# Moving the sums of the weights to earlier places in a fused attention and mixer kernel on one Trainium2 core

## The chip, the cores and the metric

The kernel runs on one core of one Trainium2 chip. The metric is the device time of one execution in microseconds (us). Five engines run side by side, each with its own in-order queue: PE (TensorE: matmuls, with weight loads shown as PEld), DVE (VectorE), ACT (ScalarE), POOL (GpSimd) and SP (SyncE), which here only issues DMAs.

## The reference, cut to what matters

```python
def _attn_ref(q, k, v, mem_k, mem_v):             # q, k, v: 4 x 8 x 768 x 64
    for c in range(24):                           # chunks of 32 queries
        k_full = concat(mem_k, k[c_start - 16 : c_end + 8])   # 8 memory keys first
        a = softmax(q_c @ k_full.T / 8)           # denominator + 1e-9
        out[:, :, c_start:c_end] = a @ v_full

def _moe_ref(x, U, V, w_ch1, w_ch2):              # x: 4 x 768 x 512
    h = x.transpose(0, 2, 1) @ U @ V              # rank 32 over the sequence
    u = x + h.transpose(0, 2, 1)
    ch = np.maximum(u @ w_ch1, 0.0) @ w_ch2       # 512 -> 2048 -> 512
    return u + ch
```

The output of the attention, with its heads laid side by side, is the input x of the mixer. U, V, w_ch1 and w_ch2 arrive as 64-bit floats.

## The kernel before, in words

The four batches run one after another. A batch's mixer has two blocks of 384 tokens. The 2048 hidden columns are cut in 16 units of 128 (f = 0 to 15), two of which make a pair p. Each product is done in three passes over high and low parts of its operands (names ending in h and l), so a unit costs twelve matmuls into a hidden bank (`ps_h`), then a split of the ReLU of the bank into `hh` (ACT, L1254 or L1414) and `hl` (DVE, L1255 or L1415), then `w2_step`: six matmuls with hh and three with hl into the accumulators `acc`. There are two hidden banks and two buffers each of hh and hl.

**Batch 0** is plain: 32 units in `both_blocks`. The weights are decoded during it, each unit's w1 to a high part `w1h` that stays in SBUF and a low part `w1l` that is written to DRAM (`w1s`, `w1x`) and fetched again by SP when wanted, into a ring of five tiles. The last six units (n = 26 to 31) are f = 15, 14, 10, 11, 12, 13 of block 1.

**Batches 1 to 3** use a seven-product scheme in the manner of Strassen (`sevens`): for a pair, seven products of half size serve both blocks. It needs sums and differences of quarters of w1, the weights' sums, four for each pair, made once and kept in DRAM. `keep_sums` makes them from two whole w1 tiles: `whole` (POOL, L453) adds w1h and w1l of each, POOL does four additions (L463), ACT casts each of the four results to a high part (L466) and DVE subtracts to get the low part (L467); `save_sums` then lets SP write the four tiles to DRAM (L472). The tiles `homes` of a pair are the same as those of the pair ahead, so a cast can only write when the DMA that saved the pair ahead has landed.

**Where the sums are made before.** In batch 1, pairs 0 to 4 (`NPL = 5`) run their first block's product plain (the loop over `few = 10` units: `half_of`, the second half, the split, the `w2_step` of the unit ahead), since their sums do not exist yet. Beside it `late_sums` makes the sums of pairs 5, 6 and 7: it fetches their w1l again from DRAM into `vbs[1]` and works there. Pairs 5 to 7 then run as seven products. In the second half of batch 1, `other_half` adds two products to what was kept for each of the ten plain units, and makes the sums of pairs 0 to 4 from the very tiles that it multiplies with (`both`, L453 on `w1l`). The second half ends with w2 units alone.

**What else runs beside.** `attention(b + 1)` is a generator whose pieces (transposes of kn and qn, scores `kall,qt`, exponentials `pt`, transposes `ident,pt`, products `vb,pT`, the rank-32 chain) are put between the mixer's steps by calls of `give`. When they are used up, `give` takes pieces of `seven_u(b + 1)`, which turns the next batch's x (`ident,x`) into `uc` and makes the operands bh, bl, t12, t34 and b22 from it. For batch 1 these pieces are taken by hand near the end of the plain loop.

**What sets the order.** PE and SP run in the order in which the program is written. ACT, DVE and POOL are put in order by the framework's scheduler, except in marked stretches.

The lines that matter most below:

```python
if few:
    half_of(0)
    for _ in gen[0]: pass          # the last pieces of batch 1's attention
    ...
    for f in range(few):           # second half, split, half_of(f + 1), w2_step of the unit ahead
        ...
        if f == 0: last_step()     # w2_step of batch 0's last unit
        else: w2_step(b, 0, *prev, go)
```

Of the kernel before, what the change touches and what calls it, by code (L numbers as in the profile page):

```python
# [45 lines left out]
LASTW = 13  # L46
RING = 4
# [10 lines left out]
def chunk_attn_then_mixer_kernel(  # L58
# [418 lines left out]
    def late_sums():  # L477

        work = vbs[1].rearrange("c i d -> c (i d)")
        lows = [work[:, 512 * n:512 * n + 512] for n in range(2)]  # L480

        def fetch(p):
            for n in range(2):
                load_w1l(2 * p + n, lows[n].rearrange("p (c n) -> p c n", c=NCK))

        def make(p):
            for n in range(2):
                whole(lows[n], w1h[2 * p + n].rearrange("p c n -> p (c n)"), lows[n])
            keep_sums(p, *lows, [work[:, 1024:1536], work[:, 1536:2048]] + [slot([P, 512], F32, "sums") for _ in range(2)])

        for p in range(NPL, NF // 2):
            for step in (fetch, None, make, None, None, None):
                if step is not None:
                    step(p)
                yield
            save_sums()
# [697 lines left out]

    def list_items(b):
# [33 lines left out]
    def sevens(b, give, following, last_step=None):  # L1229
# [44 lines left out]
        prev, more = None, late_sums() if few else iter(())  # L1274

        def go():
            give()
            next(more, None)

        if few:  # L1280
# [11 lines left out]
            for f in range(few):  # L1292
                if f == 1:
                    send()
                six(banks[f], w1h[f][:, 2:4], lows.pop(f)[:, 1], 1, False)
                h = split(banks.pop(f)[:, :TOK])
# [5 lines left out]
                if f + 2 == few:  # L1302
                    closing.enter_context(tc.manual_schedule(engines=CLOSING))
                for _ in range(max(0, min(2, f + 4 - few))):
                    next(coming[0])
                go()
                if f + 1 < few:
                    half_of(f + 1)
                if f == 0:
                    last_step()  # L1310
                else:
                    w2_step(b, 0, *prev, go)
                if f + 3 >= few:
                    next(coming[0])
                prev = (f, 0, f == 0, None) + h
            for _ in more:
                pass
            held_w.close()
            seven["pools"][1].append(ctx.enter_context(tc.tile_pool(name="su2", bufs=1, side="right", reuse_waits="tile")))
        for p in range(few // 2, NF // 2):  # L1320
# [5 lines left out]
            last = p + 1 == NF // 2  # L1326
            xb, yb = hidden_bank(), hidden_bank()
# [291 lines left out]
```

## Time and profile before

| | us |
|---|---|
| median of 3 runs | 664.64 (664.52 to 665.15) |
| the profiled execution | 663.14 |
| its span, first to last instruction | 661.4 |
| PE busy | 635.6 (96%) |
| DVE, ACT, POOL busy | 362.3, 249.5, 84.6 |

PE is busy in all but a few stretches, so the time is the sum of PE's work and of the moments when PE has to wait. A wait on another engine matters only where PE is late because of it. In batch 0's last units, batch 1's plain part and its second half (170 to 380 us) the waits of PE can be read one by one; from 380 us to the last units PE does not wait.

### The profile page before, as it was taken

The numbers are of one execution on the slowest core, as the hardware profiler recorded it, in microseconds if no ns is written. First come the engines' busy times: TensorE is split into PE (matmuls) and PEld (weight loads), VectorE is DVE, ScalarE is ACT, GpSimd is POOL, SyncE is SP. The second block draws the span as 40 slices with busy tenths as digits, with TensorE's granted clock in tenths as the row PEclk, the third lists the DMA queues.
The fourth block names the chain that finished last, engine by engine and source line by source line (L and its number), as shares of the span: only waits on it lengthen the run. The fifth ranks groups of instructions, "written<-read, shape, count | busy, mean of one in ns | idle before, by whom it ended". The sixth has DMA issues, their size and how long they took to land.

```text
span 661.4 us, 15256 instructions
## 1 busy us (share of the span) xinstructions
PE 635.6 (96%) x6171; PEld 552.7 (84%) x6174; DVE 362.3 (55%) x703; ACT 249.5 (38%) x605; POOL 84.6 (13%) x114
## 2 busy tenths in 40 slices
PE   7698999999899999999999999999999999999997
PEld 5557999988787897898788699999978899999886
DVE  5948788898654536644577733443536732222322
ACT  5526344457323365533233516342224512122221
POOL 5100000042000335101666000000000000000000
PEclk9899999999999999999999999999999999999999
DMA  8994577765572696846565369675523046555301
GB/s 242 171 365 153 170 248 246 222 188 142 98 176 55 190 264 193 212 135 167 178 221 185 134 206 279 202 183 150 150 60 128 1 145 185 156 159 160 105 0 49
DMA packets 127150, 110.32 MB, mean 167 GB/s; under 512 B 51720, under 2 KB 97928, under 8 KB 127080
## 3 DMA queue, kind: packets, MB, share of 16 engines
q1 hardware_dynamic: 126456, 109.20, 57.1%
q8 instruction: 49, 0.80, 0.5%
q10 hardware_dynamic: 624, 0.15, 0.1%
q14 instruction: 21, 0.17, 0.1%
HBM read 86.11 MB, written 22.68 MB: 164 GB/s over the span
## 4 chain that ended last, share of the span: by engine, by line
PE 63%; DMA 4%; DVE 4%; ACT 2%; issue 1%; POOL 1%; SPq 0%; ACTq 0%; DVEq 0%; POOLq 0%
PE ps_h L1240 25%; PE acc L1457 18%; PE acc L1467 9%; PE ps_a L715 2%; DMA w1s<-both 2%; PE ps_h L1406 2%; PE acc L1451 2%; PE ps_a L583 1%; PE ps_a L696 1%; PE ps_a L642 1%; PE ps_a L1139 1%; DMA vb<-w1s 1%; DMA vb<-in_v_dram 1%; PE ps_a L1044 1%; PE ps_a L744 1%
## 5 line engine op out<-in xcount | busy, mean ns | idle before, releaser
L1457 PE MATMUL acc<-w,hh 128*128 128x512 f32 x612 | 158.5, 394 | 2.2 <-ACT hh L1254 2.2
L1457 PEld LDWEIGHTS acc<-w,hh 128*128 128x128 f32 x612 | 112.9, 188 | 23.0 <-ACT hh L1254 3.3
L1467 PE MATMUL acc<-w,hl 128*128 128x512 f32 x306 | 88.0, 396 | 0.0
L1467 PEld LDWEIGHTS acc<-w,hl 128*128 128x128 f32 x306 | 56.3, 188 | 11.9 <-DVE hl L1255 0.4
L1240 PE MATMUL ps_h<-t12h,w1l 128*128 128x384 f32 x192 | 57.1, 348 | 1.0 <-DMA w1l<-w1s 1.0
L1240 PE MATMUL ps_h<-bh,w1l 128*128 128x384 f32 x192 | 52.6, 339 | 0.0
L1240 PE MATMUL ps_h<-t34h,w1l 128*128 128x384 f32 x152 | 46.6, 348 | 0.0
L1406 PE MATMUL ps_h<-uh,w1h 128*128 128x384 f32 x124 | 42.5, 347 | 2.2 <-ACT w1h L365 1.2
L1255 DVE SCALAR_TENSOR_TENSOR hl<-ps_h,hh 128x384 fp32r<-128x384 f32 x29 | 16.1, 555 | 46.7 <-ACT hh L1254 46.7
L1406 PE MATMUL ps_h<-ul,w1h 128*128 128x384 f32 x124 | 41.3, 337 | 0.4 <-DVE ul L1121 0.4
L1262 DVE TENSOR_TENSOR c<-ps_h,c 128x384 f32<-128x384 f32 x19 | 10.6, 557 | 56.8 <-PE ps_h L1240 56.8
L1240 PEld LDWEIGHTS ps_h<-t12h,w1l 128*128 128x128 f32 x192 | 35.3, 188 | 3.3 <-DVE hst L1262 1.9
L1240 PEld LDWEIGHTS ps_h<-bh,w1l 128*128 128x128 f32 x192 | 35.1, 188 | 0.8
L1240 PE MATMUL ps_h<-b,w1l 128*128 128x384 f32 x174 | 35.3, 338 | 0.0
L1254 ACT ACTIVATE hh<-ps_h 128x384 fp32r<-128x384 f32 x29 | 14.3, 494 | 53.3 <-PE ps_h L1240 51.9
L1262 DVE TENSOR_TENSOR hst<-ps_h,hst 128x384 f32<-128x384 f32 x36 | 19.9, 553 | 24.5 <-ACT hst L1266 19.4
L1255 DVE SCALAR_TENSOR_TENSOR hl<-hst,hh 128x384 fp32r<-128x384 f32 x36 | 21.1, 585 | 22.2 <-PE acc L1467 21.4
L1254 ACT ACTIVATE hh<-hst 128x384 fp32r<-128x384 f32 x36 | 18.9, 525 | 36.0 <-PE acc L1457 30.1
L1240 PE MATMUL ps_h<-t12l,w1l 128*128 128x384 f32 x96 | 32.4, 337 | 0.0
L1266 ACT COPY c<-ps_h 128x384 f32<-128x384 f32 x19 | 9.1, 480 | 61.1 <-PE ps_h L1240 61.1
L1240 PEld LDWEIGHTS ps_h<-b,w1l 128*128 128x128 f32 x174 | 30.8, 188 | 0.3 <-DMA w1l<-w1s 0.3
L1414 ACT ACTIVATE hh<-ps_h 128x384 fp32r<-128x384 f32 x31 | 15.2, 490 | 40.5 <-PE ps_h L1406 40.5
(240 smaller groups left out, 1258.9 us busy)
## 6 DMA issues: line engine op xcount, KB each, us to landing
w1l<-w1s SPq DMA_DIRECT2D x155, 256.0 KB
rw<-in_moe_w_ch_dram SPq DMA_DIRECT2D x14, 512.0 KB
qraw<-in_q_dram SPq DMA_DIRECT2D x24, 256.0 KB
out_dram<-x SPq DMA_DIRECT2D x24, 256.0 KB
vb<-in_v_dram SPq DMA_DIRECT2D x56, 98.0 KB
raw<-in_moe_w_ch_dram SPq DMA_DIRECT2D x20, 256.0 KB
w1s<-both SPq DMA_DIRECT2D x20, 256.0 KB
kraw<-in_k_dram SPq DMA_DIRECT2D x16, 256.0 KB
```

What stands on the lines that cost most here:

```text
L583: nc.tensor.transpose(out=psv[:, p, r, :], in_=half[:, r, 2 * p:2 * p + 2, :].rearrange("n h d -> n (h d)"), identity=ident,)
L715: nc.tensor.matmul(out=psv[g][CK * i:CK * i + CK, t, j], lhsT=pt[j % 2][rows, 2 * t + j // 2, CK * i:CK * i + CK], rhs=vt[rows, NI * t + i ...
L1240: nc.tensor.matmul(out=ps[:, :TOK], lhsT=w_, rhs=u, start=(start and m == 0), stop=(m == 5), skip_group_check=True,)
L1254: nc.scalar.activation(out=hh, in_=c, func=AF.Relu)
L1255: nc.vector.scalar_tensor_tensor(out=hl, in0=c, scalar=0.0, in1=hh.bitcast(F32), op0=ALU.max, op1=ALU.subtract,)
L1262: nc.vector.tensor_tensor(out=out, in0=ps[:, :TOK], in1=in1, op=ALU.add)
L1266: nc.scalar.copy(out=out, in_=ps[:, :TOK])
L1406: nc.tensor.matmul(out=ph[:, :TOK], lhsT=w[:, c, :], rhs=u[c], start=(m == 0), stop=(m + 1 == len(parts)),)
L1414: nc.scalar.activation(out=hh, in_=ph[:, :TOK], func=AF.Relu)
L1451: nc.tensor.matmul(out=acc[tt], lhsT=h[:, sl], rhs=w, start=False, stop=(m == 2))
L1457: nc.tensor.matmul(out=acc[tt], lhsT=h[:, sl], rhs=w, start=(begins and m == 0), stop=False,)
L1467: nc.tensor.matmul(out=acc[tt], lhsT=hl[:, sl], rhs=w2h[f], start=False, stop=ends is not None)
```

## The change

The table below says how the sums are spread. In the last six units of batch 0 and in the plain loop, `take_value` makes the whole tile right behind the unit's products, from the w1l that the unit has used, and calls `keep_sums` when both units of a pair are there. Nothing is fetched again for it. A ring tile of w1l is now also read by POOL before it can be filled again.

| pairs | sums made before | sums made now |
|---|---|---|
| 7, 5, 6 | plain part of batch 1 (`late_sums`) | last six units of batch 0 |
| 0, 1, 2, 3 | second half of batch 1 (`other_half`) | plain part of batch 1 |
| 4 | second half of batch 1 | second half of batch 1, first |

The saves of a pair's sums are issued when the next pair is complete. Batch 1's second half takes its units in another order (15, 8, 9, 0 to 7, 10 to 14). At batch 1's head `last_step` comes first, then two halves instead of one. There is one call of `give` fewer ahead of the plain loop's end and the calls in pairs 5 to 7 stand at other places, so pieces of the attention move by one place. The pieces of `seven_u(1)` are taken in other units (`NEXTS`). Batch 1's first three output tiles are sent at n == 2 of the second half instead of when they are ready.

```diff
+NEXTS = {3: (1, 1), 2: (2, 3), 1: (1, 1)}
...
-    def late_sums():
...
+    def take_value(f, w1l, homes):
+        p, odd = divmod(f, 2)
+        values[f] = homes(f % 2)
+        whole(values[f], *(w.rearrange("p c n -> p (c n)") for w in (w1h[f], w1l)))
+        if 2 * p in values and 2 * p + 1 in values:
             save_sums()
+            keep_sums(p, values.pop(2 * p), values.pop(2 * p + 1), [homes(2 + n) for n in range(4)])
+    def slot_home(n):
+        return slot([P, 512], F32, "sums")
+    def work_home(n):
+        return vbs[1].rearrange("c i d -> c (i d)")[:, 512 * n:512 * n + 512] if n < 4 else slot_home(n)
...
+    def others(few):
+        return list(range(few - 2, few)) + list(range(few - 2)) if few else []
...
+            def other(f):
+                low = lows.pop(f)
+                six(banks[f], w1h[f][:, 2:4], low[:, 1], 1, False)
+                if f < few - 2:
+                    take_value(f, low.rearrange("p i c n -> p (i c) n"), work_home)
+                return split(banks.pop(f)[:, :TOK])
+            last_step()
             half_of(0)
+            half_of(1)
             for _ in gen[0]:
                 pass
             gen[0] = attention(b + 1, xs)
-            for f in range(few):
+            prev = (0, 0, True, None) + other(0)
+            for f in range(1, few):
+                h = other(f)
...
-                if f + 2 == few:
+                if f + 1 == few:
                     closing.enter_context(tc.manual_schedule(engines=CLOSING))
-                for _ in range(max(0, min(2, f + 4 - few))):
+                early, late = NEXTS.get(few - f, (0, 0))
+                for _ in range(early):
                     next(coming[0])
-                go()
+                give()
                 if f + 1 < few:
                     half_of(f + 1)
-                if f == 0:
-                    last_step()
-                else:
-                    w2_step(b, 0, *prev, go)
-                if f + 3 >= few:
+                w2_step(b, 0, *prev, give)
+                for _ in range(late):
                     next(coming[0])
+                if f + 2 == few:
+                    save_sums()
...
             for z in range(2):
                 w = product(ps, 6 if z else 3, z == 0)
-                at = slice(2 * P * z, 2 * P * z + 2 * P)
-                whole(both[f % 2][:, at], *(w[:, n].rearrange("p c n -> p (c n)") for n in range(2)))
+                if f + 2 >= few:
+                    ...
...
-        for n, f in enumerate([NF - 1] + list(range(NF - 1))):
+        for n, f in enumerate(order):
             hid_ = split(kept(f))
...
+            if n == 2:
+                save_sums()
+                send()
...
-            if not (SEVEN <= b + 1 < B and t + TB >= NT):
+            if b != SEVEN and not (b + 1 < B and t + TB >= NT):
                 send()
...
             hid_ = w1_step(0, blk, f, w1l, between if n else joins)
+            if blk and f >= 2 * NPL:
+                take_value(f, w1l, slot_home if f >= NF - 2 else work_home)
```

On PE, at the place where batch 0 ends and batch 1 begins. Before (hl: last pass of unit 30's w2; w1h_877: unit 0's weights; g,v: the rank-32 chain of batch 1's attention):

```order
L1467 MATMUL acc_2683<-w_1869,hl 128x512
L1240 MATMUL ps_h<-bh,w1h_877 128x384
L1240 MATMUL ps_h<-bl,w1h_877 128x384
L1240 MATMUL ps_h<-bh,w1h_877 128x384
L1240 MATMUL ps_h<-bl,w1h_877 128x384
L1240 MATMUL ps_h<-bh,w1l 128x384 x2
L1044 MATMUL ps_a<-g_2920,v_111 128x512 x3
L1240 MATMUL ps_h<-bh,w1h_877 128x384
```

On PE at the same place now (w_1961: the w2 of batch 0's last unit):

```order
L1474 MATMUL acc_2703<-w_1869,hl 128x512
L1464 MATMUL acc_2701<-w_1961,hh 128x512 x2
L1464 MATMUL acc_2702<-w_1961,hh 128x512 x2
L1464 MATMUL acc_2703<-w_1961,hh 128x512 x2
L1474 MATMUL acc_2701<-w_1961,hl 128x512
L1474 MATMUL acc_2702<-w_1961,hl 128x512
L1474 MATMUL acc_2703<-w_1961,hl 128x512
L1240 MATMUL ps_h<-bh,w1h_877 128x384
```

The nine matmuls of batch 0's last w2 step now stand between unit 30's w2 and batch 1's first half, the first reader of bh and bl.

On ACT at that place. Before (g: the rank-32 chain; uc, bh: operands of batch 1; hst: the kept half):

```order
L1026 CAST g_2920<-ps_a 96x512
L1141 COPY uc<-ps_a 128x512
L1145 CAST bh<-uc 128x4x128
L1414 ACTIVATE hh<-ps_h 128x384
L1141 COPY uc<-ps_a 128x512
L1145 CAST bh<-uc 128x4x128
L1141 COPY uc<-ps_a 128x512
L1145 CAST bh<-uc 128x4x128
L1266 COPY hst_3022<-ps_h 128x384
```

On ACT now (vb_115 and sums: the homes of a pair's sums, here pair 6, then pair 0):

```order
L1023 CAST g_2960<-ps_a 96x512
L467 CAST vb_115<-vb_115 128x256 x2
L1138 COPY uc<-ps_a 128x512
L467 CAST sums<-vb_115 128x256 x2
L1142 CAST bh<-uc 128x4x128
L1421 ACTIVATE hh<-ps_h 128x384
L1138 COPY uc<-ps_a 128x512
L1142 CAST bh<-uc 128x4x128
L1138 COPY uc<-ps_a 128x512
L1142 CAST bh<-uc 128x4x128
L467 CAST sums<-vb_115 128x256 x2
L1266 COPY hst_3082<-ps_h 128x384 x2
```

Six casts of sums now stand among the operands of batch 1, two of them ahead of the first uc.

On SP, in the second half of batch 1. Before (out_dram: batch 1's first three output tiles; w1l: ring tiles to come):

```order
L1199 DMA w1l<-w1s_126 128x512
L1432 DMA out_dram<-x 128x512 x3
L1199 DMA w1l<-w1s_127 128x512 x2
L1199 DMA w1l<-w1x_135 128x512
L1199 DMA w1l<-w1s_127 128x512
```

On SP now:

```order
L1199 DMA w1l<-w1s_127 128x512 x2
L1199 DMA w1l<-w1x_135 128x512
L1199 DMA w1l<-w1s_127 128x512
L473 DMA w1s_130<-both 128x512 x4
L1439 DMA out_dram<-x 128x512 x3
L1199 DMA w1l<-w1s_128 128x512 x2
```

The output tiles are sent eight ring tiles later (four of pair 4 stand ahead of those of pair 0), behind the saves of pair 4's sums.

## Rows read from the trace of the kernel before

**Rows 1.** Windows: us, busy PE PEld DVE ACT POOL (x count), PE clock, DMA, GB/s

```profile
170.00:205.00 35.00, 33.87 (x659) 27.63 (x658) 16.84 (x38) 8.85 (x19) 1.62 (x5) 1.00 0.63 135
220.00:250.00 30.00, 30.00 (x166) 27.20 (x165) 12.71 (x26) 15.12 (x47) 8.79 (x11) 1.00 0.84 244
358.00:374.00 16.00, 13.78 (x61) 10.16 (x60) 15.63 (x32) 8.97 (x21) 4.88 (x6) 1.00 0.58 197
490.00:532.00 42.00, 42.00 (x200) 34.75 (x199) 26.64 (x53) 18.30 (x35) 0.00 (x0) 1.00 0.15 51
```

**Rows 2.** Waits of PE: us in total, times, longest

```profile
PE ps_a L696 <- ACT pt L668: 2.5, 2, 1.6
PE acc L1457 <- ACT hh L1254: 2.2, 3, 1.1
...
PE ps_h L1240 <- DMA w1l<-w1s: 1.0, 1, 1.0
...
PE ps_h L1240 <- ACT bh L1145: 0.6, 1, 0.6
...
PE ps_h L1240 <- DVE bl L1129: 0.3, 1, 0.3
```

**Rows 3.** Timeline of ACT and DVE at batch 1's head: start, us, what

```profile
214.93 0.62 ACT L1145 CAST bh<-uc 128x512 fp32r<-128x512 f32 x1
215.57 0.69 DVE L1129 TENSOR_TENSOR bl<-uc,bh 128x512 fp32r<-128x512 f32 x1 [1.08 <-ACT bh L1145]
```

**Rows 4.** The chain that ended last, two pieces of batch 2: start, us

```profile
388.24 1.36 PE acc L1457 x6
390.28 2.10 PE ps_h L1240 x12
```

**Rows 5.** Timeline round the first exponentials of batch 2's attention

```profile
252.49 1.48 PE L642 MATMUL ps_a<-kall,qt 64*32 64x64 f32 x128
...
259.36 0.41 ACT L466 CAST vb<-vb 128x256 fp32r<-128x256 f32 x1 [3.62 <-POOL vb L463]
...
260.35 0.66 PE L696 MATMUL ps_a<-ident,pt 128*128 128x128 f32 x4 [1.60 <-ACT pt L668]
```

**Rows 6.** Timeline of PE round the third exponentials of batch 2's attention

```profile
302.79 1.49 PE L642 MATMUL ps_a<-kall,qt 64*32 64x64 f32 x128
...
307.47 0.66 PE L696 MATMUL ps_a<-ident,pt 128*128 128x128 f32 x4 [0.93 <-ACT pt L668]
```

**Rows 7.** Timeline of SP in the second half of batch 1

```profile
319.42 1.86 SPq L1432 DMA_DIRECT2D out_dram<-x  x3
```

**Rows 8.** Timeline of DVE and POOL near the end of batch 1

```profile
360.36 2.67 POOL L463 TENSOR_TENSOR both<-both 128x256 f32<-128x256 f32 x3
...
360.61 0.95 DVE L1167 TENSOR_TENSOR tb<-uc 128x256 f32<-128x256 f32 x1
...
369.54 0.41 DVE L1167 TENSOR_TENSOR tb<-uc 128x256 f32<-128x256 f32 x1
```

**Rows 9.** Groups by line and form: busy us, mean ns, idle before

```profile
...
L467 DVE TENSOR_TENSOR both<-both 128x256 fp32r<-128x256 f32 x20 | 10.3, 527 | 7.3 <-ACT both L466 7.2
...
L463 POOL TENSOR_TENSOR vb<-vb 128x256 f32<-128x256 f32 x12 | 9.2, 766 | 0.9
...
L466 ACT CAST both<-both 128x256 fp32r<-128x256 f32 x20 | 8.1, 405 | 17.6 <-DMA w1s<-both 12.2 <-POOL both L463 5.4
...
L453 POOL TENSOR_TENSOR vb<-w1h,vb 128x512 f32<-128x512 f32 x6 | 8.0, 1341 | 44.3 <-DMA vb<-w1s 44.3
```

**Rows 10.** Timeline of SP and POOL at batch 1's head: fetches and their reader

```profile
205.98 0.42 SPq L444 DMA_DIRECT2D w1l<-w1s  x1
...
214.96 0.42 SPq L444 DMA_DIRECT2D vb<-w1s  x1
...
217.59 2.56 POOL L453 TENSOR_TENSOR vb<-w1h,vb 128x512 f32<-128x512 f32 x2 [19.68 <-DMA vb<-w1s]
```

**Rows 11.** The chain, a piece of batch 1's second half

```profile
350.18 4.82 DMA w1s<-both
```

More of the change, by code (lines that the diff above doesn't have):

```diff
@@ L475, in save_sums @@
         unkept.clear()
-    def late_sums():
[L479 to L495, printed above, removed]
-            save_sums()
+    values = {}
+    def take_value(f, w1l, homes):
[3 more added lines that the diff above has]
+        if 2 * p in values and 2 * p + 1 in values:
+            save_sums()
+            keep_sums(p, values.pop(2 * p), values.pop(2 * p + 1), [homes(2 + n) for n in range(4)])
[3 more added lines that the diff above has]
+        return vbs[1].rearrange("c i d -> c (i d)")[:, 512 * n:512 * n + 512] if n < 4 else slot_home(n)
     def attention(b, xs):
@@ L1211, in list_items @@
         items.extend(whole_item(w1s_d[p][:, n]) for p in range(few // 2, NF // 2) for n in range(7))
-        for f in range(few):
+        for f in others(few):
             p, odd = divmod(f, 2)
@@ L1272, in hidden_bank @@
             return ps_h.tile([P, 512], F32, name="ps_h")
[L1274 to L1278, printed above, removed]
+        prev = None
         if few:
@@ L1291, in sevens @@
             gen[0] = attention(b + 1, xs)
-            for f in range(few):
+            prev = (0, 0, True, None) + other(0)
+            for f in range(1, few):
+                h = other(f)
                 if f == 1:
                     send()
-                six(banks[f], w1h[f][:, 2:4], lows.pop(f)[:, 1], 1, False)
-                h = split(banks.pop(f)[:, :TOK])
                 if f + 3 == few:
@@ L1326, in sevens @@
             last = p + 1 == NF // 2
+            even, other_places = (give, lambda: None) if few else (lambda: None, give)
             xb, yb = hidden_bank(), hidden_bank()
@@ L1330, in sevens @@
             keep(c11, xb)
+            even()
             product(yb, 1, True)
@@ L1334, in sevens @@
             if prev is not None:
-                next(coming[0])
+                for _ in coming[0]:
+                    pass
                 w2_step(b, 0, *prev)
                 prev = None
-                for _ in coming[0]:
-                    pass
                 coming[0] = seven_u(b + 1)
                 closing.close()
-            go()
+            other_places()
             product(xb, 2, False)
             keep(c12, xb)
-            go()
+            give()
             product(yb, 3, True)
-            go()
+            other_places()
             product(xb, 4, False)
@@ L1350, in sevens @@
             add(c22, yb, c22)
-            w2_step(b, 0, 2 * p, 0, 2 * p == 0, None, *h1, go)
-            go()
+            even()
+            w2_step(b, 0, 2 * p, 0, 2 * p == 0, None, *h1, other_places)
+            give()
             product(xb, 5, False)
@@ L1357, in sevens @@
             add(c12, yb, c12)
-            go()
-            w2_step(b, 0, 2 * p + 1, 0, False, True if last else None, *h2)
+            give()
+            w2_step(b, 0, 2 * p + 1, 0, False, True if last else None, *h2, even)
         if few:
@@ L1368, in other_half @@
                 w = product(ps, 6 if z else 3, z == 0)
-                at = slice(2 * P * z, 2 * P * z + 2 * P)
-                whole(both[f % 2][:, at], *(w[:, n].rearrange("p c n -> p (c n)") for n in range(2)))
+                if f + 2 >= few:
+                    at = slice(2 * P * z, 2 * P * z + 2 * P)
+                    whole(both[f % 2][:, at], *(w[:, n].rearrange("p c n -> p (c n)") for n in range(2)))
             add(kept(f), ps, kept(f))
-            if f % 2:
-                save_sums()
+            if f + 1 == few:
                 keep_sums(f // 2, both[0], both[1], both[2:])
-        for f in range(min(2, few)):
+        left = others(few)
+        order = [NF - 1] + left + list(range(few, NF - 1))
+        for f in left[:2]:
             other_half(f)
             give()
-        for n, f in enumerate([NF - 1] + list(range(NF - 1))):
+        for n, f in enumerate(order):
             hid_ = split(kept(f))
@@ L1386, in sevens @@
             if n + 2 < few:
-                other_half(n + 2)
+                other_half(left[n + 2])
                 if n < LATER:
@@ L1391, in sevens @@
                 w2_step(b, 1, *prev)
-            if n == 2 * LATER:
-                save_sums()
             prev = (f, 0, n == 0, True if n == NF - 1 else None) + hid_
```

4 lines of the change are left out of this document (1 added, 3 removed).

## The prediction

> **What bounds the kernel now.** I began with the page's busy shares: PE is busy 96% of the span, so the time is PE's work plus the moments in which PE stands. Then I read the granted clock in the windows, which is 1.00 in every stretch quoted [rows 1], the level of 2.4 GHz, so that no part of the time is a matter of the clock. Then came PE's waits from batch 1's head (205 us) to its end (374 us): the reader is to see that there are only a handful, 6.6 us together, each with its releaser [rows 2]: 2.5 for exponentials, 2.2 for splits, 1.0 for a fetch, 0.9 for the operands bh and bl. Last came the timelines round each of them. In batch 0's last units PE is busy 33.87 of 35 us, so another 1.1 us of waits stands there; what ends them (decodes of weights) is not touched, and I leave them in. From batch 2 on nothing is changed: PE's work is the same, and its waits start after the stretch.
>
> The profiled execution took 663.14 us (span 661.4, 1.74 around it); the median of the runs is 664.64, 1.50 above it. I make the sum against 663.14 and carry the 1.50 over.
>
> **What it removes and adds.** No matmul is added or removed; moved ones keep their length. So the time moves by PE's waits alone, and the gain can't be over the 6.6 us. Of other engines' work, six fetches for pairs 5 to 7 go (vb<-w1s, SP issue 0.42 us each [rows 10]). The sums themselves are only moved: for a pair four ACT casts of 0.405 us (1.6), four DVE subtractions of 0.527 (2.1), on POOL two wholes of 1.34 and four additions of 0.77 (5.8) [rows 9]. Three pairs come into batch 0's last units: 4.9 us of ACT, 6.3 of DVE, 17.2 of POOL, where in 35 us ACT leaves 26 idle, DVE 18 and POOL 33 [rows 1]; they are hidden as long as no single one stands ahead of a split. The plain part has four pairs in place of three: 1.6 more on ACT, 2.1 on DVE, 5.8 on POOL, where in 30 us ACT leaves 15, DVE 17 and POOL 21 [rows 1]. The second half loses four of its five pairs.
>
> **Term 1, the head: −0.6.** PE waits 0.6 for bh and 0.3 for bl, since batch 1's first half comes straight behind unit 30's w2 and bl is only ready at 216.26 (215.57 + 0.69) [rows 2, 3]. Now last_step stands ahead, a w2 step of nine matmuls: from 388.24 to 390.28, 2.04 us [rows 4]. That covers the 0.9, and also some 0.5 by which bl may be late, because two casts of sums (0.41 each [rows 5]) stand ahead of the first uc on ACT. These casts want the saves of pair 5 landed. They are issued behind SP's fetch at 205.98, so from about 206.5 [rows 10]; landings shown are 2.2 us (217.59 less the issue's end at 215.38 [rows 10]) and 4.82 [rows 11], which gives 208.7 to 211.3, and the four issues of 0.42 lie beside it. The first uc is copied at about 211, so the cover is thin at the upper end, and the 2.04 is what hides it. I charge 0.3 for what is late next: the split of unit 0 now stands behind the output additions of last_step on DVE. So 0.9 − 0.3 = 0.6; the ends are 0 and 0.9.
>
> **Term 2, the first exponentials: −1.2.** At 260.35 the transposes of pt wait 1.60 us for ACT's exponentials, and on ACT a cast of sums stands ahead, having waited 3.62 for POOL's additions [rows 5]. POOL is late because its wholes wait for the re-fetched w1l; 19.68 us of such a wait stand at one of them [rows 10], 44.3 in all [rows 9]. These fetches are gone: the wholes now read a tile that PE has just used. What is late next is the cast, which waits for the saves of the pair ahead, landing 2.2 to 4.8 us after issue, so I leave 0.4 of the 1.6. Ends: 0 and 1.6.
>
> **Term 3, the third exponentials: −0.9.** At 307.47 the transposes wait 0.93; the scores ended at 304.28 (302.79 + 1.49), so only 3.2 us stood between [rows 6]. In the second half the exponentials now have two halves of 1.05 and a w2 step of 2.04 between (1.05 is half of a product of twelve, 2.10 [rows 4]): 4.1 us against the 3.2 with its wait of 0.93, which just covers it. Ends: 0.4 and 0.9.
>
> **Term 4, the fetch behind the sends: −1.0.** SP issues three output tiles at 319.42, which takes until 321.28 since it waits there, and the fetches of w1l stand queued behind; PE then waits 1.0 for w1l [rows 2, 7]. The sends move eight ring tiles later, where x has long been added. On SP the sends now stand behind the saves of pair 4, which wait for DVE; the queue behind these is the ring, with two more tiles ahead of need. Ends: 0.5 and 1.0.
>
> **Term 5, the splits before batch 2: −2.2.** Between 358 and 374 us DVE is busy 15.63 of 16 us [rows 1] and PE waits three times for hh, 2.2 in all [rows 2]. There seven_u(2) runs beside the sums of pairs 3 and 4, and POOL's additions slow DVE: a subtraction tb takes 0.95 beside them and 0.41 alone [rows 8]. Without these sums DVE has 8.4 us less in the second half (16 × 0.527), ACT 6.5 (16 × 0.405 [rows 9]), and POOL nothing. The nearest row without sums is the same stretch of batch 2, 490 to 532 us, where PE is busy 42.00 of 42 us and DVE 26.64 [rows 1]. Ends: 0.9 (only the longest hh wait, 1.1, half gone, and one other) and 2.2.
>
> **New waits: +1.0.** No row of before shows sums beside batch 0's last units or four pairs in the plain part. Below, the bound is nothing: both stretches have idle time enough. A gain is excluded, since waits can't fall under the 0.0 that PE has there beside those counted. Above, each of five places (three pairs in the tail, two of the plain part's pairs that stand next to exponentials) costs 0.73, the mean of the three hh waits (2.2 / 3), 3.7 for all. By the nearer row, the plain part's window with PE busy 30.00 of 30 while three pairs' sums run [rows 1], it is close to nothing; I take 0.2 a place, 1.0.
>
> Sum: −0.6 − 1.2 − 0.9 − 1.0 − 2.2 + 1.0 = −4.9; 663.14 − 4.9 = 658.2, and with the 1.50 it is 659.7. The likeliest case's own range: all waits gone, −6.6, gives 658.0; the other end takes the middle between the terms' low ends (0 + 0 + 0.4 + 0.5 + 0.9 = 1.8) and their 5.9, less the 1.0: −2.8, or 661.8.
>
> **The skill against it.** A subtraction on DVE with both inputs in SBUF takes 0.41 us alone and 0.95 beside POOL [rows 8]. The Trainium skill ("SBUF — State Buffer", section "Who interferes with whom") says that GpSimd's only SBUF ports are those of DVE's second pair, held exclusively by one of them at a time; the 0.95 agrees. By that rule POOL's 23 us in the plain part could stall DVE for as long, in small pieces, where I charge almost nothing; this is rival D below.
>
> **Rivals.**
> A. The stage of batch 2's operands stays crowded: the order of units leaves one unit fewer for seven_u(2), so the 2.2 of term 5 remain. For it: DVE's 15.63 of 16; against it: POOL's and the sums' part of this goes. −2.7: 661.9. Chance 0.11.
> B. The waits of terms 2 to 4 come back one piece later, because the pieces that consume moved as well as those that produce. For it: the distance from scores to transposes in the plain part stays about what it was. Then only terms 1 and 5 count, less the 1.0: −1.8: 662.8. Chance 0.11.
> C. ACT is held up in the plain part by casts that wait for saves: terms 1 and 2 give nothing, and each of four pairs costs 0.73 in place of the 1.0: −4.1 + 2.9 = −1.2: 663.4. For it: the casts of the second half waited 12.2 us for w1s<-both [rows 9]; against: saves now have a pair's whole time. Chance 0.08.
> D. POOL holds DVE up at eight wholes in the plain part, 0.54 (0.95 − 0.41) each, and the delay reaches PE through hl: 4.3 of the 4.9 lost: 664.0. Against it: hl has six matmuls of hh before it is wanted, and in 220 to 250 us PE did not wait beside 8.79 us of POOL [rows 1]. Chance 0.05.
> E. Slower: saves land too late for the pairs' rhythm. In the plain part a pair comes every two units: 2 × (1.05 + 1.05 + 2.04), with a piece of scores of 1.48 [rows 5], 9.8 us. Issue 0.42, landing L, a cast of 0.41 and four subtractions of 2.1 must fit in, as the next casts write the same homes: from L of 6.9 us each pair makes PE wait. The DMA engines are busy .84 there [rows 1]; at L of 8.9 it is 2 us a pair, four pairs 8 us, with terms 3 to 5 kept (−4.1): 664.64 + 3.9 = 668.5. Against it: the 4.82 of the row, and fewer fetches. Chance 0.13.
>
> **How the numbers follow.** The forecast has the remaining 0.52. A measurement of this kernel tells 0.2% from nothing, 1.33 us: faster is under 663.31, slower over 665.97. The forecast, A, most of B (0.08) and half of C make faster: 0.52 + 0.11 + 0.08 + 0.04 = 0.75. E less a small part is slower, 0.12. The rest is same, 0.13. The range reaches from all waits gone, 657.9, to D's 664.0, and leaves out E and a few in a hundred below.
>
> **What would show it.** In the profile after, PE's waits between 205 and 374 us have no row on bh or bl at the head (term 1), none of the transposes of pt on exponentials (2, 3), none on w1l behind the sends (4), and none on hh before batch 2, with DVE under 14 of 16 us there (5). New rows would be splits in batch 0's last units or the plain part. I am wrong if ACT's casts wait in the plain part for the saves over 7 us (E) or PE's rows on hh or hl stand there in number (C, D), or if the waits on exponentials keep their 2.5 (B).

## The result and the profile after

The changed kernel takes 657.88 us (median; 656.83 to 658.78) beside 664.89 us for the kernel before on the same chip: ratio 0.9886, interval 0.9856 to 0.9915, a gain of 7.0 us. The forecast was 659.7 us, 4.9 us less, with a range from 657.9 to 664.0: the direction was right, the size too small, and the time lies a hair under the range.

The profiled execution of after has a span of 657.0 us, 4.4 us under the 661.4 of before; the rest of the 7.0 lies in how executions scatter (below). PE's waits from batch 1's head to its end, in the same view as [rows 2]:

```profile
PE ps_h L1240 <- DVE hl L1255: 0.5, 1, 0.5
PE ps_h L1240 <- ACT hst L1266: 0.4, 1, 0.4
```

None of the five rows of [rows 2] is left: no exponentials, no hh, no fetch, no bh or bl. Two new rows stand there, for hl and for a kept half, 0.9 us together (a third gap, of 0.07 us, is too short for the view to list). The windows that answer to [rows 1] (batch 0's last units, the plain part, the stretch before batch 2, batch 2's second half) read:

```profile
170.00:205.00 35.00, 32.65 (x651) 26.91 (x653) 23.47 (x47) 11.53 (x27) 16.95 (x21) 1.00 0.67 167
222.00:252.00 30.00, 29.52 (x162) 26.50 (x161) 14.99 (x30) 15.92 (x49) 15.55 (x17) 1.00 0.90 277
353.50:369.50 16.00, 16.00 (x85) 13.59 (x84) 11.26 (x26) 9.79 (x19) 0.00 (x0) 1.00 0.15 43
486.00:528.00 42.00, 42.00 (x200) 34.79 (x199) 26.72 (x54) 18.30 (x35) 0.00 (x0) 1.00 0.15 51
```

In the third, DVE falls from 15.63 to 11.26 us of 16, POOL from 4.88 to nothing, and PE has no gap. In the first, DVE rises from 16.84 to 23.47 and POOL from 1.62 to 16.95 us, as sums are made there now, and PE loses 1.2 us more than before. That is one stop, which the prediction does not have. The rows of PE and SP round it, in the timeline of after:

```profile
195.05 4.10 SPq L473 DMA_DIRECT2D w1s<-sums  x4
...
197.60 1.38 PE L712 MATMUL ps_a<-vb,pT 64*32 64x64 f32 x108
...
200.19 0.41 PE L712 MATMUL ps_a<-vb,pT 64*32 64x64 f32 x20 [1.21 <-issue]
```

PE breaks off after 108 of 128 products of the attention and waits for nothing that the profile names ("issue"); the four saves of pair 7's sums run just ahead.

**A ruler for everything that follows.** The two traces are aligned best at the w2 step of batch 0's unit 30 (PE, 212.21 us in before, 214.72 in after), the last work that is the same in both. From there to the end of the span it is 449.15 us in before and 442.27 in after: the change is worth 6.9 us in this stretch of these two executions. Ahead of it after is 2.5 us later, of which 1.2 are the stop and 1.1 stand already at the first w2 step (58.84 and 59.91 us), before anything that was changed. All kernels, in profiled executions, with the median of the timed runs and the ratio to the kernel before on the same chip (all in us; the stop is PE's idle time behind product 108):

| kernel | to unit 30's w2 | from there to the end | PE's listed gaps there | stop at 200 us | median | ratio (interval) |
|---|---|---|---|---|---|---|
| before | 212.21 | 449.15 | 6.6 | 0 | 664.89 | 1 |
| b_again | 214.52 | 450.42 | 7.7 | 0 | 666.16 | 1.0012 (0.9998 to 1.0026) |
| after | 214.72 | 442.27 | 1.0 | 1.21 | 657.88 | 0.9886 (0.9856 to 0.9915) |
| a_again | 212.98 | 442.31 | 1.0 | 0 | 657.08 | 0.9893 (0.9873 to 0.9913) |
| a_third | 213.12 | 443.49 | 1.7 | 0.48 | 657.65 | 0.9888 (0.9869 to 0.9908) |
| a_send | 213.73 | 442.32 | 1.2 | 1.02 | 657.99 | 0.9901 (0.9884 to 0.9919) |
| a_head | 214.59 | 446.14 | 2.9 | 1.48 | 661.24 | 0.9951 (0.9934 to 0.9968) |
| a_second | 213.21 | 445.40 | 2.9 | 1.21 | 660.41 | 0.9932 (0.9909 to 0.9956) |
| a_double | 213.19 | 451.71 | 7.5 | 0.39 | 667.79 | 1.0047 (1.0029 to 1.0065) |
| b_tail | 213.45 | 448.09 | 5.8 | 0.39 | 663.81 | 0.9988 (0.9972 to 1.0005) |
| a_late | 215.24 | 442.27 | 1.3 | 0.11 | 657.10 | 0.9888 (0.9868 to 0.9908) |
| a_best | 213.68 | 442.51 | 1.9 | 0.11 | 658.23 | 0.9891 (0.9868 to 0.9914) |
| a_send_pieces | 216.51 | 440.94 | 0.6 | 1.76 | 657.99 | 0.9876 (0.9845 to 0.9908) |
| a_send_give | 212.10 | 445.91 | 4.6 | 0 | 659.44 | 0.9910 (0.9881 to 0.9940) |
| a_give | 215.62 | 444.22 | 3.0 | 0.93 | 661.21 | 0.9934 (0.9912 to 0.9955) |
| a_best2 | 214.16 | 440.51 | 0.5 | 0.38 | 656.07 | 0.9862 (0.9833 to 0.9890) |

### The profile page after: what moved, and what is told of

It is laid out like the page before. It is cut to its first block, busy times and chain, and to the rows that moved or that the text cites. A ratio compares the mean times of both kernels' runs of the same rounds, so it can differ in the third digit from the quotient of the medians.

```text
span 657.0 us, 15205 instructions
## 1 busy us (share of the span) xinstructions
PE 636.0 (97%) x6171; PEld 552.2 (84%) x6174; DVE 362.2 (55%) x703; ACT 249.5 (38%) x605; POOL 80.8 (12%) x106
## 4 chain that ended last, share of the span: by engine, by line
PE 69%; DVE 3%; POOL 1%; issue 0%; DMA 0%; ACT 0%; ACTq 0%
PE ps_h L1240 27%; PE acc L1464 20%; PE acc L1474 10%; PE ps_a L712 2%; PE acc L1458 2%; PE ps_a L580 2%; PE ps_h L1413 2%; PE ps_a L639 1%; PE ps_a L1136 1%; PE ps_a L693 1%; PE ps_a L741 1%; DVE x L1429 1%; PE ps_a L1041 1%; PE ps_a L1018 0%; DMA w1l<-w1s 0%
```

## The experiments

**The two kernels again** (a_again, a_third, b_again; no edit).

> The changed kernel unaltered, profiled and timed once more. Theory A (the gain is PE's waits inside batch 1, and what lies ahead of batch 1 only scatters from one execution to the next): from the start of batch 0's last but one w2 step (unit 30) to the end of the span again 442.3 us (within 0.3), while the stretch ahead of it, 214.72 us in the first profile, comes out anywhere between 211.5 and 215.5, and the 1.21 us stop of PE at 200 us inside the vb,pT products, which waits for nothing that the profile shows, is gone or elsewhere; ratio to before 0.9886 to 0.9905. Theory B (the stop at 200 us is a new price of the saves in batch 0's last units): it stands there again with 1.0 us or more.

> The kernel before, unaltered. Theory A: from the start of unit 30's w2 step to the end again 449.1 us (within 0.3; 449.15 in the first profile), and the stretch ahead of it, 212.21 us in the first profile, scatters by 1 to 2 us, which is the 1.5 between the profiled time and the median; ratio 0.998 to 1.002. Theory B (that stretch is a fixed part of each kernel): it is 212.2 again within 0.2.

> The changed kernel unaltered, beside the improved one on the same chip: 442.3 us from unit 30's w2 step to the end, the three waits of 0.98 us in it; the stop at 200 us there or not, as it was in three of four kernels with these saves; ratio to before 0.987 to 0.991.

From unit 30 on, after gave 442.31 and 443.49, before 450.42. So waits scatter from one execution to the next: in b_again the views list 2.9 us for exponentials (2.5 in [rows 2]), 2.5 for splits (2.2) and 0.4 for a kept half, and a_third has 0.9 us of kept halves. The expectations of 449.1 within 0.3 and of 442.3 in a_third missed by 1.3 and 1.2. The gain from unit 30 on is 6.9 by the first pair of profiles, 8.1 by the second and 7.1 by the means of the two and the three. The stop at 200 us is gone in a_again, as its theory A has it, and 0.48 in a_third. Over the eleven profiled executions in this document that save pair 7's sums there, it is 0 twice and 0.39 to 1.76 nine times, 0.8 in the mean. In the kernel before no view lists it, but in b_again products 108 and 109 start 0.20 us apart, where 0.01 is usual. So theory B of a_again is right in kind: the new place has its price, paid most times. What sets it is taken up at the end.

**Term 4: the sends** (a_send): the output tiles go when they are ready, and no longer at n == 2.

```diff
                 save_sums()
-                send()
...
-            if b != SEVEN and not (b + 1 < B and t + TB >= NT):
+            if not (SEVEN <= b + 1 < B and t + TB >= NT):
```

> The changed kernel with batch 1's first three output tiles sent when they are ready, as before, and not at n == 2 of the second half. Theory A (term 4: the sends hold up the fetches of w1l queued behind them): a wait of PE for w1l of 0.8 to 1.2 us comes back behind the sends, from unit 30's w2 step to the end 443.1 to 443.5 us, ratio to before 0.990 to 0.992. Theory B (the wait went because no saves of pairs 0 to 3 stand in the second half any more, so that the fetches have room): no wait, 442.3 us, as the changed kernel.

No wait for w1l, 442.32 us: moving the sends back alone costs nothing, against my theory. Here the additions to x run at 313.69 us and SP sends at 314.40, so nothing is held up. Two more tries followed: the calls of give in pairs 5 to 7 at the old places as well,

```diff
-            even, other_places = (give, lambda: None) if few else (lambda: None, give)
+            even, other_places = lambda: None, give
```

> The changed kernel with the early sends, and with the calls of give in pairs 5 to 7 at the places of before, so that each piece of batch 2's attention comes one place later there. Theory A (term 4, second form: the sends were late in the kernel before because the additions to x stood on DVE behind the multiplications of the attention, 315.31 to 316.73 us, which wait for vb,pT, and behind a subtraction of the sums; the fetches of w1l queue behind the sends): the additions start 2 us or more after block 0's last matmul, the sends and the fetches behind them are late, and PE waits 0.5 to 1.6 us for w1l; and PE's second wait for pt (0.9 us, at 307 in the kernel before) is back, since it belongs to the same places: 443.5 to 445.0 us from unit 30's w2 step to the end against 442.3. Theory B (it was the saves or the order of units): no wait for w1l, 442.3 to 443.0.

which gave no wait either (and a shorter stretch, 440.94, to which I come back); and two more calls of give at the end of the plain loop, which put DVE's queue at this place back to what it was before, once with the early and once with the late sends:

```diff
-            held_w.close()
+            [give() for _ in range(2)]; held_w.close()
```

> The changed kernel with the early sends and two more calls of give at the end of the plain loop, so that on DVE the attention's multiplications (x from ps_a and rs) and one subtraction of pair 4's sums stand ahead of the three additions to x again, one more subtraction between them, word for word as in the kernel before. Theory A (term 4: sends that wait for late additions hold up the fetches behind them): the additions run 2 to 4 us after block 0's last matmul, the sends end as late, and PE waits 0.6 to 1.6 us for w1l. Theory B (the fetches have slack all the same): no such wait.

> The same two calls of give, with the late sends of the changed kernel. Theory A: the additions are as late, but nothing on SP waits for them, so no wait of PE for w1l; what is over the changed kernel's 442.3 us is the shifted pieces' alone. Theory B (the late additions themselves or the pieces' places make the wait): it is there as in the kernel with early sends.

That brought it back. The timeline of a_send_give (DVE, SP, PE):

```profile
314.65 1.42 DVE L723 TENSOR_TENSOR x<-ps_a,rs 128x256 f32<-128x256 f32 x4 [0.17 <-PE ps_a L712]
...
317.36 0.63 DVE L468 TENSOR_TENSOR both<-both 128x256 fp32r<-128x256 f32 x1 [1.28 <-ACT both L467]
317.91 0.68 DVE L1428 TENSOR_TENSOR x<-acc,x 128x512 f32<-128x512 f32 x1
...
318.61 2.24 SPq L1438 DMA_DIRECT2D out_dram<-x  x3
...
320.95 0.90 SPq L1199 DMA_DIRECT2D w1l<-w1s  x2
...
324.10 0.41 PE L1240 MATMUL ps_h<-t12h,w1l 128*128 128x384 f32 x1 [1.10 <-DMA w1l<-w1s]
```

The additions to x (L1428) stand on DVE behind the attention's multiplications and behind a subtraction that waits for ACT; the sends wait for them, the fetches queue behind the sends, and PE waits 1.10 and then 0.54 us more for w1l. In a_give the additions are as late (321.93 us), but nothing on SP waits for them, and no such row is listed; its stretch is 1.7 us shorter. So the wait of before needed both the early sends and the late additions, and the change took away both: with either one alone (a_send, a_give) PE does not wait. What this is worth in time is less sure, as the medians lie the other way (659.44 for a_send_give, 661.21 for a_give). Both also have a wait of 0.8 us for kn and a stop of 1.56 us behind 104 of 128 products of scores (`kall,qt`), which after and a_send do not have.

**Term 1: the head** (a_head).

```diff
-            last_step()
             half_of(0)
+            last_step()
             half_of(1)
```

> The changed kernel with batch 1's first half ahead of the last w2 step of batch 0, as before (the second half of the two behind it). Theory A (term 1: the w2 step covers bl): PE waits 0.9 to 1.6 us for bh and bl at the first half, more than before since casts of sums stand ahead of uc on ACT, and the 0.48 us wait for hl at 225 us goes or stays; 442.9 to 443.6 us from unit 30's w2 step to the end. Theory B (the operands are ready by then whatever the order): 442.3 or less.

It cost 3.9 us, not 0.6 to 1.3. The timeline of a_head at the head, and the window behind it:

```profile
217.04 2.45 DVE L1126 TENSOR_TENSOR bl<-uc,bh 128x512 fp32r<-128x512 f32 x2
...
217.98 0.44 PE L1240 MATMUL ps_h<-bh,w1h 128*128 128x384 f32 x1 [0.62 <-ACT bh L1142]
219.55 0.44 PE L1240 MATMUL ps_h<-bl,w1h 128*128 128x384 f32 x1 [1.13 <-DVE bl L1126]
...
220.60 2.76 PE L1464 MATMUL acc<-w,hh 128*128 128x512 f32 x6
```

```profile
220.40:223.80 3.40, 3.40 (x10) 2.73 (x9) 1.05 (x2) 0.91 (x3) 1.80 (x2) 0.50 0.02 5
```

The waits are 0.62 and 1.13 us: bl takes 1.22 us apiece beside POOL's additions (0.69 in [rows 3]). The rule of the Trainium skill that the prediction named ("SBUF — State Buffer", section "Who interferes with whom") agrees, and here it reached PE. Behind the two waits the granted clock falls to 0.50, the 1.2 GHz level, until 223.8 us, and the w2 step after them takes 2.76 us for its six matmuls in place of 1.36 [rows 4]. So last_step in front is what makes room for the sums at this place; without it more than half of the change's gain would have gone. What needs the room is POOL's work for pair 0, the first pair of the plain part, and not the sums of batch 0's last units: b_tail, below, makes the latter in the old order of the head, and its waits for bh and bl are those of before.

**Term 5 and the plain part** (a_second, a_double). In a_second the sums of pairs 0 to 3 are made in other_half again, for every unit, and not in `other`:

```diff
-                if f < few - 2:
+                if False:
                     take_value(f, low.rearrange("p i c n -> p (i c) n"), work_home)
...
-                if f + 2 >= few:
+                if True:
...
-            if f + 1 == few:
+            if f % 2:
+                save_sums()
                 keep_sums(f // 2, both[0], both[1], both[2:])
```

> The changed kernel, but the sums of pairs 0 to 3 made in the second half again and not in the plain part. Theory A (terms 4 and 5: these sums held up the operands of batch 2 and the fetches): PE's waits for hh at batch 2's operands come back, 2.2 to 2.5 us, and the wait for w1l of 1.0 us too, though the sends stay late, since the send alone did not bring it back; from unit 30's w2 step to the end 445.0 to 446.0 us against 442.3. Theory B (the waits went by the new order of units and pieces): 442.3 to 443.0. Either way the plain part, now without sums, shows what they cost there: nothing by my forecast's nearest row, so its stretch is not shorter than the changed kernel's by over 0.5 us; by rivals C and D it would be 2.9 to 4.3 us shorter.

It is 3.1 us longer, but in other parts than expected: one wait of 2.33 us, then a fall of the clock, and no wait for w1l. Its seven timed runs lie between 657.3 and 663.0 us, so this may not come in each. PE, ACT and a window of a_second:

```profile
361.22 0.40 ACT L467 CAST both<-both 128x256 fp32r<-128x256 f32 x1 [5.45 <-DMA w1s<-both]
...
363.14 0.52 ACT L1254 ACTIVATE hh<-hst 128x384 fp32r<-128x384 f32 x1
```

```profile
363.71 2.40 PE L1466 MATMUL acc<-w,hh 128*128 128x512 f32 x6 [2.33 <-ACT hh L1254]
```

```profile
364.40:367.80 3.40, 3.40 (x11) 2.64 (x10) 3.40 (x11) 2.50 (x7) 0.00 (x0) 0.50 0.72 237
```

ACT stood 5.45 us in a cast that waited for the save of the pair ahead, with the split queued behind. 3.4 us at half the clock are 1.7 us of work lost. The plain part without the sums is 0.7 us shorter: by that much the distance from unit 30 to the end of it (the w2 step that starts at 265.91 us in after) is less in a_second. Nearly all of this is the wait for hl at 225 us, which cost 0.65 (below) and which a_second does not have. So the sums of four pairs cost 0.7 us there, and rivals C and D, at 2.9 and 4.3, are out. But that place is nearly full: a_double makes the wholes, casts and subtractions of these pairs twice.

> The changed kernel with the sums of pairs 0 to 3 made with twice the work in the plain part: eight more wholes on POOL (10.9 us), sixteen more casts on ACT (6.5 us) and sixteen more subtractions on DVE (8.4 us), the results the same. Theory A (the plain part has that room): at most 1.0 us more, 442.3 to 443.3 from unit 30's w2 step to the end. Theory B (rivals C and D: the plain part is at its edge and each whole holds up a split): eight times 0.5, 446.3 or more.

Theory A had at most 1.0 us; it is 9.4 us more, on theory B's side. The waits of PE in a_double from 205 to 376 us (three largest of five rows):

```profile
PE ps_a L583 <- DVE kn L532: 3.2, 2, 2.7
PE ps_h L1243 <- DVE hl L1258: 1.2, 1, 1.2
PE ps_a L696 <- ACT pt L668: 1.2, 1, 1.2
```

DVE is latest with the keys of the next attention (kn), where the argument had looked at the splits, and the clock falls behind the wait of 2.67 us (0.50 from 251.6 to 255.0). The 14 to 15 us in 30 for which DVE, ACT and POOL are each idle in the window of after above were no room of that size. The second cast of a tile also has to wait for the first subtraction, which reads that tile, so a_double lengthens each pair's chain and not the work alone; the two are not told apart.

**Term 2 alone** (b_tail): the kernel before with `take_value` in batch 0's last units in place of `late_sums`, and the last pair's saves behind the first `send()` of the plain loop.

> The kernel before with one part of the change alone: the sums of pairs 7, 5 and 6 in batch 0's last six units, nothing fetched again in the plain part. Theory A (term 2: the first exponentials stand behind casts that wait for POOL and the fetches): PE's first wait for pt of 1.6 to 2.0 us goes to under 0.4, the others stay; from unit 30's w2 step to the end 447.6 to 448.5 against 449.15 and 450.42 of the kernel before. At the head casts now stand among bh and bl as in the changed kernel, so the waits there grow from 0.9 to 1.7 us, and the clock may fall as where batch 1's first half was put ahead of the w2 step, which would be 1.7 more. Theory B (the wait comes of the distance from scores to transposes): it stays at 1.6 or more.

The row of [rows 5], in the timeline of b_tail:

```profile
260.28 0.66 PE L692 MATMUL ps_a<-ident,pt 128*128 128x128 f32 x4 [0.29 <-ACT pt L664]
```

1.60 has become 0.29, by this part of the change alone; the second wait for pt stays at 0.89. The stretch is 448.09, 1.1 to 2.3 us under the two profiles of before, though the wait for w1l is 1.61 in place of 0.99. The waits for bh and bl did not grow, against the expectation:

```profile
PE ps_h L1236 <- ACT bh L1141: 0.6, 1, 0.6
PE ps_h L1236 <- DVE bl L1125: 0.3, 1, 0.3
```

The clock stays at 1.00, POOL does nothing from 212 to 224 us and bl takes 0.69 us: the casts of batch 0's last sums cost nothing there with the old order of the head. By the median the ratio is 0.9988, no difference that can be told from none.

**The stop at 200 us** (a_late, a_best, a_best2). In a_late pair 7's saves are issued one unit later:

```diff
-            save_sums()
+            (f == 2 * NPL + 1) or save_sums()
...
-        values[f] = homes(f % 2)
+        values[f] = homes(f % 2) if f != 2 * NPL + 2 else (save_sums(), homes(f % 2))[1]
```

> The changed kernel with the saves of pair 7's sums issued behind the next fetch of w1l, one unit later, some 7 us on. Theory A (the four saves at 195 us hold up the block of PE's instructions fetched beside them, and PE stops after 108 of the 128 vb,pT products): no stop there, up to 1.2 us less ahead of batch 1, ratio to before 0.987 to 0.989. Theory B (the stop has nothing to do with the saves): it is seen again, or pair 5's casts wait for the later saves and hold up a split: same time or up to 1 us more.

The 128 products stand in one row now and the saves start at 202.53 us:

```profile
198.84 1.91 PE L712 MATMUL ps_a<-vb,pT 64*32 64x64 f32 x128
...
200.33 0.25 PEld L712 LDWEIGHTS ps_a<-vb,pT 64*32 64x32 f32 x20 [0.27 <-issue]
...
202.53 1.95 SPq L473 DMA_DIRECT2D w1s<-sums  x4
```

But the weight loads still break off behind the 108th, and products 108 and 109 start 0.33 us apart, with 0.11 us of idle time that the view merges: the stop is shorter, not gone. A wait of 0.38 us (PE for g, at 210.84) comes in return, and the median is that of a_again. a_best adds to it the casts of t34 ahead of batch 1's first seven products:

> The changed kernel with pair 7's saves one unit later, as in the run before, and the casts of t34 (operands of batch 1's first seven products) ahead of the first of these products instead of behind the second. Theory A: the wait for the kept half (0.43 and 0.07 us listed at 276 us, 0.93 us by the starts of the matmuls) goes, since ACT is idle from 269.8 to 274.0: 441.2 to 441.6 us from unit 30's w2 step to the end against 442.3, and no stop at 200 us; ratio to before 0.985 to 0.988. Theory B (the casts, now ahead of the first product's copy on ACT and DVE, make that copy and the additions late): as much is lost again, 442.3 or more.

The wait for the kept half at 276 us went, but there are waits of 0.49 us for another kept half at 246.68, of 0.35 at 270.48 with no releaser named, and of 0.58 for a copy on ACT at 289.21: 442.51, on theory B's side. The first two stand in a_late too, with 0.29 and 0.24, so they are not all the casts' doing. a_best2 takes the late saves and the old places of give that had done well in a_send_pieces:

> The changed kernel with the calls of give in pairs 5 to 7 at the places of before, early sends, and pair 7's saves one unit later. Theory A (the places of before cost 1.4 us less than the new ones, as seen once, and the stop at 200 us belongs to the saves): 440.7 to 441.3 us from unit 30's w2 step to the end, at most 0.2 us of stop at 200 us and no fall of the clock after it, ratio to before 0.984 to 0.987. Theory B (the 440.9 was one good execution): 442.0 or more.

PE's waits in it from 205 to 376 us:

```profile
PE ps_h L1240 <- DVE hl L1255: 0.5, 1, 0.5
PE ps_a L1041 <- DVE g L1024: 0.4, 1, 0.4
```

440.51 us, the shortest stretch of all, with no fall of the clock at 200 us. The stop there is 0.38, though the saves are late; expected was at most 0.2. Its median, 656.07 us, is the lowest too, 1.8 us under the changed kernel's; the intervals of the two ratios overlap, so by times alone it is not told from the changed kernel, while the two traces with these places of give (440.94 and 440.51) lie under all five with the new places and nothing else that bears on this stretch (442.27 to 443.49).

## Why the prediction was wrong

**The step that failed** is the ceiling: "the time moves by PE's waits alone, and the gain can't be over the 6.6 us". The low end of the range was made from it (664.64 − 6.6, written once as 658.0 and once as 657.9). That time moves by PE's waits held; that 6.6 us is their price did not. The view lists a wait from the modelled end of one matmul to the start of the next, but matmuls overlap. PE at the head of before:

```profile
216.32 0.44 PE L1240 MATMUL ps_h<-bl,w1h 128*128 128x384 f32 x1 [0.28 <-DVE bl L1129]
216.60 0.34 PE L1240 MATMUL ps_h<-bh,w1h 128*128 128x384 f32 x1
216.78 0.33 PE L1240 MATMUL ps_h<-bl,w1h 128*128 128x384 f32 x1
```

Without a wait a matmul starts 0.18 us after the one ahead (216.60 to 216.78). The first row started 0.73 us after the one ahead of it (215.59 [0.62]), so the wait listed as 0.28 cost 0.55. From start to start, less the usual distance of such a pair, the eight waits of before cost 8.0 us in place of 6.6, and the three of after 1.6 in place of 1.0. The difference is 6.4 of the measured 6.9 of the two profiles. Part of the other 0.5 stands right behind the waits (216.32 to 216.60 is 0.28 in place of 0.18); the rest was not priced. In b_again the waits cost 9.2, which is 7.6 over those of after, where the stretches differ by 8.1. The Trainium skill ("Perfetto Trace Analysis", section "Tensor Engine Instruction (MATMUL, LD_WEIGHTS)") says that the reported end of a matmul is estimated; the rows agree.

**The terms**, start to start, forecast against measured from these two traces:
- Term 1, head: −0.6. The two waits cost 1.3, the new one for hl 0.65 (at 225.19, where the forecast had it, one half later): −0.7. Right in size. The wait for hl needs the sums beside it too: a_second, with the same order of the head and no sums there, has none.
- Term 2: −1.2. About 1.7, all of it gone. The mechanism is right (b_tail, where 0.29 is left); in after the 0.4 left over for casts that wait for saves was not needed.
- Term 3: −0.9. 1.1, gone. From the start of the scores to that of the transposes it is 4.68 us in before, the wait included, 5.68 in after, and 4.99 in a_send_pieces, where these transposes do not wait either. Which places of the pieces decide it was not tried apart.
- Term 4: −1.0. 1.1, gone (1.58 less the 0.52 that follows the same `x,u_sb` products where nothing is late). The queue was right, the reason half: the sends need late additions on DVE to do harm, and the change had moved these too.
- Term 5: −2.2. 2.8, gone. DVE's crowding was one part of it; a_second shows the other, ACT's casts that wait for saves. In before both stand on ACT ahead of the waits for hh, the first ahead of the one at 363.93 us and the second ahead of the longest, at 367.43:

```profile
362.53 0.62 ACT L1145 CAST t12h<-ta 128x512 fp32r<-128x512 f32 x1 [4.50 <-DVE ta L1129]
...
364.82 0.41 ACT L466 CAST both<-both 128x256 fp32r<-128x256 f32 x1 [0.94 <-DMA w1s<-both]
```

- New waits: +1.0. 0.9 for the kept half from 276 us on, and the stop at 200 us, 0.8 in the mean, which the profile of before does not show. Neither is a split that is held up, which is what was charged.

The five terms come to −7.4 against a forecast of −5.9, and the new waits to 1.7 against 1.0: −5.6 on the first profile of before, −6.9 with b_again's waits in its place. By the stretches themselves, with the stop counted, it is −6.1 and −7.3; timed it was −7.0. That the forecast came within 2 us is in part luck, as what went and what came were both put too low.

**The second fault** was to carry the 1.50 us between the profiled execution and the median over as if it belonged to both kernels alike: in after the profiled execution lies 0.90 over the median and not 1.50 under it. The stretch from unit 30 on differs by 1.3 us between the two profiles of before and by 1.2 among the three of after, so one pair of profiles does not give the gain to a microsecond. The timed executions leave no trace, but the spans of the profiled ones show the same: 661.4 and 664.9 us for before, 657.0, 655.3 and 656.6 for after, in the mean 663.2 and 656.3, so 6.9 where the first pair alone has 4.4.

A small misreading changed nothing: of the 1.1 us of waits that the prediction set aside in batch 0's last units, half is for the output's additions on DVE and not for decodes. Both halves are in after as they were.

Of the rivals, A and B did not come: DVE has 11.26 of 16 us, and no wait came back one piece later. Of C a_third shows a trace, 0.9 us of kept halves that ACT copies late in place of 0.4, and of D the wait for hl is one; the sums cost the plain part 0.7 us in a_second's comparison. Of E there are the waits themselves: ACT's casts stand 5.8 us for saves in the plain part of after, in seven waits, the longest 2.3, where the forecast put the edge at landings of 6.9, and none of it reaches PE. So C, D and E did not come, and a_double shows how near they were.

## What to carry to other kernels

Price a wait of TensorE from start to start of its matmuls, not from the idle time listed, take off the usual distance of the very same pair, and add the half clock that may follow. The waits of one profiled execution are not a ceiling: here two of the same kernel differ by more than 1 us in the stretch that was changed. Before work is moved into a stretch with idle engines, ask which single instruction of the next stage would stand behind it, as the idle share does not tell.

## What the runs showed of the hardware that had not been expected

- Behind single waits of 1.76 us (a_send_pieces), 2.33 (a_second) and 2.67 (a_double), and behind 0.62 and 1.13 with one matmul of 0.44 us between (a_head), the granted clock was 0.50 for the next stretch, 1.7 us of work each time. Behind single waits of 1.48 (a_head, at 200 us), 1.56 (a_send_give), 1.60 (before) and 1.98 (b_again) it stayed at 1.00. What tells the two groups apart was not settled.
- PE stopped at the same place of the program, behind 108 of 128 products, in nine of eleven profiled executions with four saves beside it, for 0.39 to 1.76 us. The three with later saves (a_late, a_best, a_best2) have 0.11, 0.11 and 0.38, so the saves are not all of it. The DMA view of after from 195 to 199 us, while 1.21 MB of data move, the saves among them, has beside them

```profile
q8 instruction: 1, 0.02, 3.3%
```

  one packet of the instruction queue. By the DMA records of the sixteen traces the stop goes with the end of this packet. Where PE stops, in b_again too, product 109 starts 1.24 to 1.59 us after the packet's end, whether that is 0.2 us before the first product (b_again, stop hardly seen) or 1.7 us after it (a_send_pieces, stop of 1.76). In the three without a stop (before, a_again, a_send_give) the packet has ended 0.14 to 0.37 us before the first product. The stops of 1.56 us in a_send_give and a_give, far from these saves, end 1.59 and 1.65 us after such a packet. That fits PE waiting for a block of its instructions; which instructions the packet holds, no view shows. With the early saves the packet ends 0.7 us behind the first product in the mean, in the other five executions 0.1; why it is late in one execution and not in the next is not shown.
